# Fifteen normalising products moved from VectorE to GpSimd in a planned attention kernel, with scores two groups ahead and a new order

## The chip, the cores and the metric

The kernel runs on one core of one Trainium2 chip. The metric is the device time of one execution in microseconds. The kernel before took 671.77 us, the median of three runs (670.23, 671.77 and 672.2).

## The reference

Two independent blocks with 2048 positions, a model width of 512 and 32 heads of width 16. Their results stand side by side in the output.

```python
# A: one K and one V for all 32 heads
q = (x @ wq) as [head, position, 16];  k = x @ wk;  v = x @ wv
p = softmax(q k^T / 4)                 # 32 heads x 2048 x 2048
a = (p v) @ wo
# B: linear attention with learned features
q, k, v = x @ wqkv, by head
phi(y) = concat(softmax(y w_phi), softmax(-y w_phi))
kv = sum_s phi(k)^T v;  z = sum_s phi(k)
b = ((phi(q) kv) / (phi(q) z + 1e-6)) @ wo
out = concat(a, b)
```

## The kernel before, in words

**Block A, the large part.** The work is cut into 32 pieces `sc` (a query block of 512, a pair of heads in four row groups, the even or odd head of each pair) by 16 key blocks `kap` of 128. For each of these 512 combinations there are four score tiles `g` of 128x512, so 2048 tiles in all. TensorE makes a score tile with one matmul of 32 rows (`score`, line 1757). From there a tile goes one of two ways:

- *The ScalarE way.* Tiles are taken in groups of two, in two neighbouring PSUM banks (`next_qk`, `qk`). One activation over 128x1024 takes the exponential into the ring `PT` (`expo`, line 1824). Four such tiles are then multiplied with V by four matmuls that run side by side in four column tiles (`pv`, line 1867).
- *The VectorE way.* VectorE turns one tile at a time into 16-bit integers whose bits, read as f16, approximate the exponential (`bits`, line 1938). Four tiles make a "quad", a plane of the buffer `Z`, which has 14 planes. The approximation sums four shifted copies. GpSimd makes the second plane from the first with one 64-bit integer addition (line 1982) and the third and fourth from the first two with another one (line 2000). If GpSimd is late by the planner's reckoning (`LATE`), or near the end (`ALONE`), VectorE makes some of the planes itself (line 1985, jobs named `dS`). Each of the four planes needs four matmuls (`d_pv`, line 2036), so a quad costs TensorE 16 matmuls with V where a ScalarE quartet costs 4.

All products with V of one `sc` accumulate in PSUM bank 5, with the sum of the weights in extra columns. When an `sc` is complete, VectorE copies it out (`finish_sc`, line 1529 as "accS"), takes the reciprocal of the sums (`finish_sc2`, line 2069), the reciprocals go by DMA through DRAM into the spread-out tile `denS`, and a product normalises two `sc` at once into `On` (`finish_sc3`, line 2096; for the last even one line 2094). There are 15 such products at line 2096, one per odd `sc` below 30: 128x512 f32 times 128x512 f32 into bf16. They are jobs named `on`. The output projection, and the copying out of a piece three later, wait for them.

**Block B** is interleaved with it: projections, exponentials on ScalarE (lines 2275 and 2354), row sums and products on VectorE, and once in the middle `b_kvfin` (lines 2331 to 2346), which closes the accumulated `kv` and `z`: two products into `KVn` (line 2338) and four small ones into `KX` (line 2346).

**The order of the work.** Nothing is scheduled on the chip. At build time the class `_Fast` simulates the engines with a duration for every job (0.60 us for a VectorE tile, 0.4267 us per tile and 0.05 us for a ScalarE group, 1.135 and 2.03 us for the GpSimd additions, `ODUR` for a normalising product), picks at each step the job that can start first, and writes out one fixed instruction order for each engine. Each engine then works through its list in order and waits on semaphores. Ties and near ties are broken by priorities plus a pseudo-random amount that depends on a seed; there is one seed for each 14 us of planned time (`SEEDS`). How many tiles go to VectorE is not fixed anywhere: a VectorE score (`dq`) is issued when the rules allow it (`dq_ok`, `can_open`, `riders`). Some of these rules:

- `LOOK`: a score group `i` for ScalarE may be issued when `i <= nex + LOOK`, where `nex` is the number of exponentials issued.
- `HOLD`: a VectorE score that would not share its time on TensorE with another score is put behind other ready TensorE work unless VectorE will have been idle for `-HOLD` us at its start.
- `LAST`: in the last piece a new quad is only opened while at least this many key blocks are left.

**Locks.** An instruction added with `lock=True` on VectorE is remembered (`last_lock`), and the next locked instruction on GpSimd waits for it. GpSimd's additions are locked, as are VectorE's normalising products, its `dS` planes, the products in `b_ew`, `b_qw` and `b_kvfin`. The planner also keeps jobs in `PAIR` and GpSimd's jobs off each other in time (`paired`, `port`).

Of the kernel before, what the change touches and what calls it, by code (L numbers as in the profile page):

```python
# [1175 lines left out]
class _Fast:  # L1176
# [697 lines left out]
    def dve_quad(self):  # L1874

        for sc in (self.asc, self.asc + 1):
            if sc < 32 and ("qa", sc // 2) in self.issued and 16 - self.at[sc] - self.dt[sc] >= (self.LAST if sc == 31 else self.AHEAD) and all(("KR", sc % 2, k) in self.issued for k in range(4)):
                return sc
# [73 lines left out]
    def block(self, quad):  # L1952
# [3 lines left out]
        late = max(0.0, self.te["pool"] - self.te["dve"]) + self.pbusy + self.PDUR + self.PPAIR  # L1956
        mode = sum(late > x for x in self.LATE)
        if self.asc >= 31 and 16 - self.at[31] - self.dt[31] <= self.ALONE:
# [372 lines left out]
    def b_kvfin(self):  # L2331


        kvS, KVn, mask = self.kvS, self.KVn, self.mask
        mk = ["mask0"] + [("mask", j) for j in range(8)]
        for a in range(2):
            o = KVn.rearrange("p g (j a e) -> p a g j e", a=2, j=4)[:, a]
            self.add("dve", (lambda a, o: (lambda v: v.tensor_tensor(out=o, in0=kvS[:, :, a, 0:16].unsqueeze(2).to_broadcast([128, 8, 4, 16]),  # L2338
                                                                     in1=mask[:, a, :].unsqueeze(1).unsqueeze(3).to_broadcast([128, 8, 4, 16]), op=ALU.mult)))(a, o),
                     reads=["kvS"] + mk, writes=[("KV", a)], lock=True)  # L2340
        z = kvS[:, :, :, 16:17]
        self.add("dve", lambda v: v.tensor_scalar(out=z, in0=z, scalar1=5e-7, scalar2=None, op0=ALU.add), reads=["kvS"], writes=["kvS"])
        for sg in range(2):
            for a in range(2):
                o, i = self.kx(1 + sg, a), z[:, 4 * sg:4 * sg + 4, a, :].to_broadcast([128, 4, 4])
                self.add("dve", (lambda o, i, a: (lambda v: v.tensor_tensor(out=o, in0=i, in1=mask[:, a, :].unsqueeze(1).to_broadcast([128, 4, 4]), op=ALU.mult)))(o, i, a),
                         reads=["kvS", "KX0"] + mk, writes=[("Zc", 2 * sg + a)], lock=True)

    def b_pq(self, m, G, dc):
        return self.Wq[:, dc, G * 128:G * 128 + 128], self.BxT[:, dc, m * 512:(m + 1) * 512], [("BxT", m), ("Wq", dc)]  # L2350
# [71 lines left out]
    def b_s8c(self, st):  # L2422
# [15 lines left out]
    ACTIVE = 4.5  # L2438
    FORCE = 3.45
    SEG = 14.0  # L2440
    SEEDS = (0, 0, 123515, 372835, 67414, 19330, 290997, 497586, 506994, 1038613, 983868, 663097, 811365, 174557, 947041, 618921,
             796598, 856510, 445263, 482332, 137281, 222396, 619280, 216959, 825991, 456468, 828108, 116528, 672282, 460342, 1003417, 806511,
             80739, 543698, 705153, 314868, 260223, 835086, 464019, 411522, 111904, 658750, 941122, 672462, 101118, 679772, 19846)
    PVN = 2
    AENG, ADUR, SENG, SDUR, ONP, ODUR = 'dve', 0.6, 'dve', 1.13, 0, 0.62
    LATE = (14.0, 24.0)
    OPEN, SPARE = 2, 4
    RESV, URGE, URG2, ORD = None, 1.0, 0.8, 0.08
    PLAST, PDPV, PDQ, PPV, SAME = 0.6, 2.0, 0.4, 1.5, 0.1
# [4 lines left out]
    AMP = (0.6, 1.0, 1.4)  # L2454
    PDUR, PPAIR = 1.135, 2.03
    GS, FREE0 = (2, 2), (0, 1, 2, 3, 4, 6, 7)
    LOOK, DLA, TOL, LAG = 1, 0.3, 0.3, 0.44
    PQE, PQR, EASE = 2.2, 1.1, 0.45
    LONE, HOLD, HOLDW = 1.2, -0.4, 0.2
    PAIR = ("dS", "on", "ew")  # L2460
    LAST = 6
    ALONE = 4
    SPREAD = 5.5
    COMPANY = 4.5
# [93 lines left out]
    def seed(self, t):  # L2558

        i = int(t / self.SEG)  # L2560
        return self.SEEDS[i] if i < len(self.SEEDS) else 0

# [164 lines left out]
```

## Time and profile before

| | before |
|---|---|
| median of 3 runs | 671.77 us |
| profiled execution, its own time | 670.24 us |
| its span, first to last instruction | 668.5 us |
| granted TensorE clock | 0.999 |
| score tiles on ScalarE / on VectorE | 1340 / 708 |
| quads on VectorE | 177 |

In the rows of the profile, "x" is the number of instructions, then follow the busy time of the group in us and the mean duration of one instruction in ns, then the idle time of the engine just before them and what ended it. Consecutive instructions of one engine overlap a little, so that the busy time of a group can be less than count times mean. PE is TensorE (PEld its weight loads), DVE VectorE, ACT ScalarE, POOL GpSimd. PE's durations contain the latency of a pipelined matmul.

### The profile page before, as it was taken

What the parts mean: (1) busy time and instruction counts of PE and PEld (TensorE: products, weight loads), DVE (VectorE), ACT (ScalarE), POOL (GpSimd) and SP (SyncE); (2) the same over time, 40 slices, a digit from 0 to 9 for tenths busy, and PEclk for the clock granted to TensorE, in tenths of its full rate; (3) what the DMA queues carried; (4) which work ended last, traced back from release to release, by engine and by line L of the source; (5) the groups of instructions that cost most, each with busy time, mean ns of one, the idle gap of its engine ahead of it and who ended that gap; (6) DMA issues with size and microseconds to landing.
All of it is one profiled execution on the core that took longest, in us unless ns stands there. A gap on an engine that the chain in (4) does not pass through costs nothing.

```text
span 668.5 us, 20877 instructions
## 1 busy us (share of the span) xinstructions
PE 650.2 (97%) x9026; PEld 202.9 (30%) x9026; DVE 621.6 (93%) x1048; ACT 652.1 (98%) x742; POOL 531.4 (79%) x413
## 2 busy tenths in 40 slices
PE   8999999999999999999999999999999999999997
PEld 3332233233332233223322323233233223222232
DVE  5999999999999999999999899999978999999985
ACT  6999999999999999999999999999999999999995
POOL 5788899986778876987688898887865778878982
PEclk9999999999999999999999999999999999999999
DMA  9931000000000100000112000130210220010101
GB/s 193 158 98 26 3 11 18 3 26 4 11 19 10 50 3 12 19 3 26 31 22 57 26 26 12 29 90 15 72 51 26 73 58 26 11 49 11 26 2 37
DMA packets 45552, 24.12 MB, mean 36 GB/s; under 512 B 35404, under 2 KB 41548, under 8 KB 45452
## 3 DMA queue, kind: packets, MB, share of 16 engines
q1 hardware_dynamic: 43724, 22.43, 14.1%
q8 instruction: 71, 1.16, 0.7%
q10 hardware_dynamic: 1728, 0.30, 0.2%
q14 instruction: 29, 0.24, 0.1%
HBM read 10.27 MB, written 4.96 MB: 23 GB/s over the span
## 4 chain that ended last, share of the span: by engine, by line
ACT 82%; PE 14%; DVE 2%; DMA 1%; POOL 0%; issue 0%
ACT f_PT L1824 78%; PE f_ps L1757 4%; PE f_ps L2036 4%; PE f_ps L1354 3%; ACT f_ET L2354 2%; PE f_ps L1867 2%; ACT f_Ek L2275 2%; DVE f_Z L1938 1%; DMA f_AxT<-in_A_x_dram 1%; PE f_ps L2123 0%; POOL f_Z L2000 0%; PE f_ps L1523 0%; DVE f_KR L1709 0%; PE f_ps L1692 0%; DVE f_KVn L2338 0%
## 5 line engine op out<-in xcount | busy, mean ns | idle before, releaser
L1824 ACT ACTIVATE f_PT<-f_ps 128x1024 bf16<-128x1024 f32 x670 | 622.8, 1137 | 3.3 <-PE f_ps L1757 1.7
L1938 DVE TENSOR_SCALAR f_Z<-f_ps 128x512 int16<-128x512 f32 x708 | 444.8, 682 | 18.9 <-PE f_ps L1757 16.1
L2000 POOL INT64_ADD f_Z<-f_Z x175 | 331.0, 1892 | 34.3 <-DVE f_On L2096 5.6
L1757 PE MATMUL f_ps<-f_QA,f_KR 32*128 32x512 bf16 x2048 | 272.5, 385 | 8.4 <-ACT f_PT L1824 5.4
L1982 POOL INT64_ADD f_Z<-f_Z x175 | 181.6, 1038 | 77.8 <-DVE f_Z L1938 47.0
L2036 PE MATMUL f_ps<-f_Z,f_VK 128*32 128x512 f16 x2832 | 229.3, 384 | 2.3 <-POOL f_Z L1982 1.4
L1757 PEld LDWEIGHTS f_ps<-f_QA,f_KR 32*128 32x128 bf16 x2048 | 74.2, 91 | 253.8 <-ACT f_PT L1824 218.5
L1867 PE MATMUL f_ps<-f_PT,f_VA 128*32 128x512 bf16 x1340 | 116.3, 385 | 0.1
L2036 PEld LDWEIGHTS f_ps<-f_Z,f_VK 128*32 128x32 bf16 x2832 | 57.2, 95 | 83.7 <-issue 56.3
L1867 PEld LDWEIGHTS f_ps<-f_PT,f_VA 128*32 128x32 bf16 x1340 | 27.5, 94 | 47.8 <-issue 42.4
L2281 DVE TENSOR_REDUCE f_ssum<-f_Ek 128x64 f32<-128x1024 bf16 x16 | 19.3, 1206 | 2.2 <-ACT f_Ek L2275 2.2
L1529 DVE COPY f_accS<-f_ps 128x512 f32<-128x512 f32 x31 | 21.1, 681 | 0.1
L2298 DVE TENSOR_TENSOR f_vS<-f_ps,f_rs 128x1024 bf16<-128x1024 f32 x16 | 19.4, 1215 | 0.5 <-PE f_ps L1354 0.5
L2354 ACT ACTIVATE f_ET<-f_ps 128x512 bf16<-128x512 f32 x32 | 19.2, 739 | 0.0
L1354 PE MATMUL f_ps<-f_Wk,f_BxT 128*32 128x512 bf16 x256 | 19.0, 383 | 0.0
L1354 PE MATMUL f_ps<-f_BxT,f_Wq 128*32 128x512 bf16 x256 | 18.5, 382 | 0.2 <-ACT f_ET L2354 0.2
L1354 PE MATMUL f_ps<-f_Bwo,f_ET 128*32 128x512 bf16 x256 | 18.6, 382 | 0.0
L1354 PE MATMUL f_ps<-f_Bwv,f_BxT 128*32 128x512 bf16 x256 | 18.5, 382 | 0.0
L2275 ACT ACTIVATE f_Ek<-f_ps 128x512 bf16<-128x512 f32 x32 | 18.3, 675 | 0.0
L1354 PE MATMUL f_ps<-f_AxT,f_wq 128*32 128x512 bf16 x240 | 17.5, 382 | 0.2 <-DVE f_Z L1938 0.2
L1523 PE MATMUL f_ps<-f_ones,f_zero 128*32 128x512 bf16 (+8 forms) x98 | 13.4, 371 | 1.3 <-POOL f_zero L1549 1.3
L1354 PE MATMUL f_ps<-f_wo,f_On 128*32 128x512 bf16 x192 | 14.3, 383 | 0.0
(106 smaller groups left out, 277.9 us busy)
## 6 DMA issues: line engine op xcount, KB each, us to landing
f_denS<-f_dd SPq DMA_DIRECT2D x15, 256.0 KB
out_dram<-f_outB SPq DMA_DIRECT2D x17, 128.0 KB, 2.6
f_Wk<-f_wd SPq DMA_DIRECT2D x4, 512.0 KB
f_Ek<-f_wd SPq DMA_DIRECT2D x4, 512.0 KB
f_accS<-f_accS SPq DMA_DIRECT2D x60, 32.0 KB
out_dram<-f_outA SPq DMA_DIRECT2D x14, 128.0 KB, 1.9
f_Bwv<-in_B_wqkv_dram SPq DMA_DIRECT2D x1, 512.0 KB
f_Bwo<-in_B_wo_dram SPq DMA_DIRECT2D x1, 512.0 KB
```

The costliest lines, as they stand in the source:

```text
L1354: mm = pe.matmul(ps[32 * j:32 * j + 32, bank, :], lhsT=l[:, 32 * j:32 * j + 32], rhs=r, start=(c == 0), stop=(c == N - 1), tile_position=( ...
L1529: self.add("dve", lambda v: v.tensor_copy(out=out, in_=in_), reads=reads, writes=writes)
L1757: return pe.matmul(self.ps[:, bank, :], lhsT=self.KR[32 * g:32 * g + 32, sc % 2, kap * 128:(kap + 1) * 128], rhs=self.QA[32 * g:32 * g + 3 ...
L1824: self.add("act", lambda a: a.activation(out=PT[:, sl[0]:sl[0] + size, :], in_=ps[:, bs[0]:bs[0] + size, :], func=ACT.Exp), reads=[("PS", ...
L1867: mm = pe.matmul(ps[32 * g:32 * g + 32, bank, :], lhsT=w, rhs=PT[:, slots[g], :], start=start, stop=stop, tile_position=(0, 32 * g))
L1938: self.add("dve", lambda v: v.tensor_scalar(out=self.Z[:, z, h, :], in0=ps[:, bank, :], scalar1=self.Z1, scalar2=self.Z0, op0=ALU.mult, op ...
L1982: self.add("pool", lambda g: g.int64_add(out=w(o), in0=w(i), in1=256 * t * 0x0001000100010001), reads=keys(z), writes=keys(p), lock=True)
L2000: self.add("pool", lambda g: g.int64_add(out=v(*o), in0=v(*sorted((z, y))), in1=512 * 0x0001000100010001), reads=keys(z) + keys(y), writes ...
L2036: mm = pe.matmul(ps[32 * g:32 * g + 32, bank, :], lhsT=w, rhs=Z[:, sl[g], :], start=start, stop=stop, tile_position=(0, 32 * g))
L2275: self.add("act", (lambda a, sg: (lambda e: e.activation(out=Ek[:, r, a].rearrange("p h f -> p (h f)"), in_=ps[:, bank, :], func=ACT.Exp, ...
L2298: self.add("dve", lambda v: v.tensor_tensor(out=vS[:, :, :, 0:16], in0=v3, in1=rs.unsqueeze(3).to_broadcast([128, 2, 32, 16]), op=ALU.mult ...
L2354: self.add("act", lambda e: e.activation(out=self.ET[:, sl, :], in_=self.ps[:, bank, :], func=ACT.Exp, scale=sg), reads=[("PS", bank)], wr ...
```

## The change

The normalising products with `sc < 30` are added to GpSimd's list in place of VectorE's (`ONP` from 0 to 30), with 1.27 us planned for one instead of 0.62. The six products of `b_kvfin` are no longer locked. Score groups may stand two ahead (`LOOK`), the thresholds `LATE`, `HOLD` and `LAST` are moved, and the seeds are new ones from the third segment on, so that the fixed order of the engines' instructions is another one.

```diff
# b_kvfin
-                     reads=["kvS"] + mk, writes=[("KV", a)], lock=True)
+                     reads=["kvS"] + mk, writes=[("KV", a)])
...
-                         reads=["kvS", "KX0"] + mk, writes=[("Zc", 2 * sg + a)], lock=True)
+                         reads=["kvS", "KX0"] + mk, writes=[("Zc", 2 * sg + a)])
# constants
-    SEEDS = (0, 0, 123515, 372835, 67414, 19330, 290997, 497586, 506994, 1038613, 983868, 663097, 811365, 174557, 947041, 618921,
...
+    SEEDS = (0, 0, 167143, 130480, 298315, 266520, 1016351, 757449, 657965, 146296, 518941, 206005, 348923, 764209, 586831, 950700,
...
-    AENG, ADUR, SENG, SDUR, ONP, ODUR = 'dve', 0.6, 'dve', 1.13, 0, 0.62
-    LATE = (14.0, 24.0)
+    AENG, ADUR, SENG, SDUR, ONP, ODUR = 'dve', 0.6, 'dve', 1.13, 30, 1.27
+    LATE = (16.0, 30.0)
...
-    LOOK, DLA, TOL, LAG = 1, 0.3, 0.3, 0.44
+    LOOK, DLA, TOL, LAG = 2, 0.3, 0.3, 0.44
...
-    LONE, HOLD, HOLDW = 1.2, -0.4, 0.2
+    LONE, HOLD, HOLDW = 1.2, -0.7, 0.2
...
-    LAST = 6
+    LAST = 8
```

The lines that read `ONP` are unchanged:

```python
self.add("pool" if sc < self.ONP else "dve", lambda v: v.tensor_tensor(out=o, in0=acc, in1=R, op=ALU.mult), reads=reads, writes=[("On", sl)], lock=True)
```

More of the change, by code (lines that the diff above doesn't have):

```diff
@@ L2440 @@
     SEG = 14.0
-    SEEDS = (0, 0, 123515, 372835, 67414, 19330, 290997, 497586, 506994, 1038613, 983868, 663097, 811365, 174557, 947041, 618921,
-             796598, 856510, 445263, 482332, 137281, 222396, 619280, 216959, 825991, 456468, 828108, 116528, 672282, 460342, 1003417, 806511,
-             80739, 543698, 705153, 314868, 260223, 835086, 464019, 411522, 111904, 658750, 941122, 672462, 101118, 679772, 19846)
+    SEEDS = (0, 0, 167143, 130480, 298315, 266520, 1016351, 757449, 657965, 146296, 518941, 206005, 348923, 764209, 586831, 950700,
+             639825, 267858, 893993, 668738, 464524, 750513, 225125, 193461, 0, 648673, 371881, 500552, 497624, 251567, 487201, 114980,
+             171633, 94996, 831771, 817116, 897134, 587649, 526128, 870704, 1011496, 896371, 868450, 261383, 0, 529598, 955066)
     PVN = 2
-    AENG, ADUR, SENG, SDUR, ONP, ODUR = 'dve', 0.6, 'dve', 1.13, 0, 0.62
-    LATE = (14.0, 24.0)
+    AENG, ADUR, SENG, SDUR, ONP, ODUR = 'dve', 0.6, 'dve', 1.13, 30, 1.27
+    LATE = (16.0, 30.0)
     OPEN, SPARE = 2, 4
```

## The prediction

> **What bounds the kernel now.** I read the page first: the busy shares, the chain that ended last, the costliest groups.
>
> ```profile
> span 668.5 us, 20877 instructions
> PE 650.2 (97%) x9026; PEld 202.9 (30%) x9026; DVE 621.6 (93%) x1048; ACT 652.1 (98%) x742; POOL 531.4 (79%) x413
> ACT 82%; PE 14%; DVE 2%; DMA 1%; POOL 0%; issue 0%
> L1824 ACT ACTIVATE f_PT<-f_ps 128x1024 bf16<-128x1024 f32 x670 | 622.8, 1137 | 3.3 <-PE f_ps L1757 1.7
> L1938 DVE TENSOR_SCALAR f_Z<-f_ps 128x512 int16<-128x512 f32 x708 | 444.8, 682 | 18.9 <-PE f_ps L1757 16.1
> L2000 POOL INT64_ADD f_Z<-f_Z x175 | 331.0, 1892 | 34.3 <-DVE f_On L2096 5.6
> L1982 POOL INT64_ADD f_Z<-f_Z x175 | 181.6, 1038 | 77.8 <-DVE f_Z L1938 47.0
> ```
>
> ScalarE carries the chain (82%) and stands only 3.3 us before its 670 score exponentials. Busy time of TensorE is no measure of its load, since the latency of pipelined matmuls is in it. Next the stretches, and the start and end of ScalarE's row in the timeline:
>
> ```profile
> core 0: us, PE busy (x) PEld busy (x) DVE busy (x) ACT busy (x) POOL busy (x), PEclk, DMA share, GB/s
> 40.00:240.00 200.00, 197.70 (x2906) 61.35 (x2898) 195.72 (x318) 199.92 (x230) 169.10 (x124) 1.00 0.06 15
> 240.00:440.00 200.00, 195.81 (x2792) 60.88 (x2792) 189.68 (x315) 197.88 (x229) 163.44 (x115) 1.00 0.10 26
> 440.00:540.00 100.00, 98.56 (x1406) 31.33 (x1396) 90.31 (x146) 99.99 (x117) 71.17 (x48) 1.00 0.20 53
> 540.00:640.00 100.00, 97.94 (x1217) 28.50 (x1219) 95.60 (x165) 99.62 (x110) 86.16 (x60) 1.00 0.08 24
> ```
>
> ```profile
> 8.36 3.91 ACT L1824 ACTIVATE f_PT<-f_ps 128x1024 bf16<-128x1024 f32 x4 [0.65 <-PE f_ps L1757]
> ```
>
> ```profile
> 649.00 9.50 ACT L1824 ACTIVATE f_PT<-f_ps 128x1024 bf16<-128x1024 f32 x10
> ```
>
> ```profile
> 562.96 72.63 ACT f_PT L1824 x79
> ```
>
> From 40 to 640 us ScalarE is busy for 597.4 of 600 us. The run is therefore a start of 8.36 us before the first score exponential, a solid block to 649.00 + 9.50 = 658.5, and a tail of 10.0 us. Only fewer exponentials shorten the block; the chain's stretch of 79 gives 72.63 / 79 = 0.92 us for each. VectorE is the engine that can take them over: it is full from 40 to 240 us (195.72 of 200), and has 2 to 10% left later. One quad more on VectorE is four score tiles, or two exponentials: **1.84 us less on ScalarE**. That is the exchange rate of this forecast.
>
> **The change, part by part.**
>
> *The products leave VectorE.*
>
> ```profile
> L2096 DVE TENSOR_TENSOR f_On<-f_accS,f_denS 128x512 bf16<-128x512 f32 x15 | 14.3, 954 | 0.0
> ```
>
> ```profile
> L2096 DVE TENSOR_TENSOR f_On<-f_accS,f_denS x15: 679/686/1957, 71.5 to 645.3; 128x512 bf16<-128x512 f32 x15
> ```
>
> VectorE is rid of 14.3 us. At the median of 686 ns the fifteen would be 10.3 us; the other 4.0 us belong to a few that took up to 1957 ns. [...]
>
> What the freed time buys: a VectorE tile costs 444.8 / 708 = 0.628 us, a quad 2.51. A quad also shortens the run by 1.84 us, and with it VectorE's own room by 93% of that, 1.71 us. So 14.3 us buy 14.3 / (2.51 + 1.71) = 3.4 quads, or 6.2 us; 10.3 us buy 2.4 quads, or 4.5 us. The order, however, is laid out with the planner's figures, 0.62 us for a product and 0.60 for a tile: 9.3 / (2.40 + 1.71) = 2.3. I take **two quads, 3.7 us**.
>
> *The products arrive on GpSimd.* The trace shows no two-operand product there. The nearest rows:
>
> ```profile
> L1585 POOL COPY f_wk_rep<-f_wk_raw 128x512 bf16<-128x512 bf16 x1 | 0.6, 609 | 1.6 <-DMA f_wk_raw<-in_A_wk_dram 1.6
> ```
>
> A copy of 512 elements takes 0.61 us; an addition over 512 words of 64 bits, which reads the same 4 KB of each partition as two f32 operands, 1.04; one over twice as much 1.89. I take 1.2, nearest to the 1.04 with a second stream to fetch, and keep 0.61 to 1.89. [...]
>
> ```profile
> POOL f_Z L2000 <- DVE f_On L2096: 5.6, 8, 0.8
> POOL f_Z L1982 <- DVE f_On L2096: 1.7, 2, 1.0
> POOL f_Z L1982 <- DVE f_KX L2346: 2.0, 1, 2.0
> POOL f_Z L1982 <- DVE f_Z L1938: 47.0, 50, 6.9
> ```
>
> GpSimd gets 15 x 1.2 = 18 us (9 to 28) and loses the locked waits on the product, 5.6 + 1.7 = 7.3 us, so some 11 us in all. Two quads bring 2 x (1.04 + 1.89) = 5.9 us. It would then be busy for 531.4 + 18 + 5.9 = 555 of about 665 us, 84%. Its slack covers that: of its idle time 47.0 us alone are spent waiting for VectorE's tiles. If the cover were gone, the following would stand behind a product: the next additions in GpSimd's list, the products with V that need their planes in TensorE's list, and behind these the scores for ScalarE. TensorE waits little for additions so far:
>
> ```profile
> PEld f_ps L2036 <- POOL f_Z L1982: 5.1, 15, 1.7
> PEld f_ps L2036 <- POOL f_Z L2000: 4.1, 15, 0.5
> ```
>
> Without any cover it would be the whole 18 us. I put the term at nothing, since the planner places a product at 1.27 us, above the price I take, and since one score group in hand covers 0.92 us.
>
> *TensorE for two more quads.*
>
> ```profile
> 299.66 1.04 PE L2036 MATMUL f_ps<-f_Z,f_VK 128*32 128x512 f16 x16
> 301.82 0.39 PE L2036 MATMUL f_ps<-f_Z,f_VK 128*32 128x512 f16 x4
> ```
>
> Four matmuls side by side follow each other at (1.04 - 0.39) / 3 = 0.22 us. A quad needs four such groups where ScalarE's quartet needs one, so 0.65 us more; two quads 1.3 us on an engine that also loses 3.7 us of span. That is 5 us, 0.7%. The order finds it from the looser `LOOK`, or it doesn't; this is the first rival.
>
> *Score groups two ahead.* The exponentials' idle time is 3.3 us in all, so this can give ScalarE no more than that. On the other side, three groups hold six of the seven banks that are free for anything but the sums. What that costs VectorE is bounded by the waits for scores it has now, 16.1 us; I take nothing for it, and leave it to the last rival.
>
> *The end.* `LAST` at 8 can leave one quad less to VectorE, 1.84 us lost. In return the end can close sooner:
>
> ```profile
> 657.15 1.89 POOL L2000 INT64_ADD f_Z<-f_Z  x1 [2.45 <-DVE f_Z L1985]
> 658.95 0.39 PE L1867 MATMUL f_ps<-f_PT,f_VA 128*32 128x512 bf16 x4
> 660.03 0.60 PE L2036 MATMUL f_ps<-f_Z,f_VK 128*32 128x512 f16 x8
> ```
>
> The last planes come from GpSimd at 659.04 and are used up at 660.63, while ScalarE's last tiles are through at 659.34: up to 1.3 us to gain. Between -1.3 and +1.8 I take nothing.
>
> *The unmarked closing.* One wait of 2.0 us on GpSimd goes. Now its addition and a product into `KVn` may collide, and VectorE may lose what it lost at line 2096, 1957 - 686 = 1.27 us, at each of two products. Once in 668 us and off ScalarE's path: nothing, at worst 2.5 us of VectorE, which is 0.6 quads or 1.1 us.
>
> `LATE` concerns planes that VectorE makes because GpSimd is late:
>
> ```profile
> L1985 DVE TENSOR_SCALAR f_Z<-f_Z x6: 679/684/1787, 649.7 to 656.4; 128x2048 int16<-128x2048 int16 x6
> ```
>
> There are six, all after 649 us, so the thresholds hardly ruled before: nothing.
>
> **The sum.** The profiled execution took 670.24 us, 1.74 more than its span. Two quads less for ScalarE: 670.24 - 3.7 = 666.5. The median of the runs lies 1.53 us above the profiled one, so for it **671.77 - 3.7 = 668.1 us**.
>
> **The rivals.**
>
> *Nothing is converted.* The products alone, by stretch:
>
> ```profile
> 40.00:240.00 200.00, 2.97 (x4) 1.00 0.06 15
> ```
>
> VectorE is relieved, but what kept quads from it after 240 us was not its own time: it had 10.3 us free from 240 to 440 and 9.7 from 440 to 540, while TensorE was as good as full. Four products fall before 240 us. Then only the 40 to 240 stretch converts, under 4 x 0.74 = 3.0 us, or 0.7 quads. The seeds may change which stalls the plan has, but ScalarE has none to give on the chip. Time: 671.77 within 1.3, so 670.5 to 673. [...]
>
> *All of it is converted.* 14.3 us for 3.4 quads, and the 1.3 us of the end: 671.77 - 7.5 = 664.3. For it speaks that the planner was wrong by 15 x (0.954 - 0.62) = 5 us on these products and is no longer; against it, that it does not know so when it lays out the order.
>
> *Slower: `HOLD` eats the gain.*
>
> ```profile
> DVE f_Z L1938 <- PE f_ps L1757: 16.1, 45, 1.6
> ```
>
> VectorE waits 45 times for a score, 0.36 us on average, which is about the 0.4 us that `HOLD` asks it to stand before a lone score. With 0.7 each wait can grow by 0.3 us: 45 x 0.3 = 13.5 us, more than the planned 9.3 that are freed. The balance of -4.2 us is one quad less (4.2 / 4.11), `LAST` takes another, and ScalarE gets four exponentials more: 671.77 + 3.7 = 675.5. It decides once these waits exceed 16.1 + 9.3 = 25.4 us. Against it: `HOLD` only reorders scores behind other ready work, and the third group gives lone scores more company to ride with.
>
> **How the numbers follow.** About 0.3%, 2.0 us, is what a measurement of this kernel can tell from no change. I give the two quads 0.47, everything converted 0.11, nothing converted 0.24, slower by `HOLD` 0.18. The forecast's own spread, a quad either way, is 666.2 to 670.0, all but its last 0.2 us beyond the bound. Faster is thus 0.58, same 0.24, slower 0.18. The range runs from 664.0, which takes in the full conversion, to 674.0, which takes in the nothing case and one quad lost; beyond lie the larger losses and a still better order.
>
> **What would show it.** In the changed profile line 1938 should have about 716 instructions in place of 708, line 1824 about 666, and line 2096 fifteen on POOL at about 1.2 us, with VectorE's busy time near 621.6 - 14.3 + 8 x 0.628 = 612 and GpSimd's near 555. ScalarE's idle time before its exponentials should stay under 5 us; if instead it grows, the products stand in front of planes (line 2036 waiting for POOL far above 9.2 us) or the banks are short. A count of 708 or less at line 1938 makes the forecast wrong at its conversion; waits of line 1938 for scores over 25 us name `HOLD`. With the counts as forecast and the time not lower, the tail or the start has grown, and the exchange rate was no rate of the whole run.

## The result and the profile after

The changed kernel takes 872.54 us, the median of six runs (869.21 to 880.52), beside 671.52 for the kernel before on the same chips: 1.300 times as long, 95% interval 1.297 to 1.303. The forecast of 668.1 was wrong in sign and by 204 us. The profiled execution took 869.21 us.

The page of the changed kernel, busy shares, chain and costliest groups:

```profile
span 867.5 us, 20854 instructions
PE 693.0 (80%) x8976; PEld 202.9 (23%) x8976; DVE 614.7 (71%) x1037; ACT 657.7 (76%) x740; POOL 553.7 (64%) x430
PE 27%; ACT 26%; issue 20%; POOL 15%; DVE 11%; DMA 1%; POOLq 0%
L1824 ACT ACTIVATE f_PT<-f_ps 128x1024 bf16<-128x1024 f32 x668 | 627.8, 1103 | 185.7 <-PE f_ps L1757 185.0
L1938 DVE TENSOR_SCALAR f_Z<-f_ps 128x512 int16<-128x512 f32 x712 | 448.8, 683 | 205.0 <-PE f_ps L1757 191.5
L2000 POOL INT64_ADD f_Z<-f_Z x176 | 333.1, 1893 | 63.7 <-issue 28.8
L2036 PE MATMUL f_ps<-f_Z,f_VK 128*32 128x512 f16 x2848 | 250.7, 410 | 149.3 <-POOL f_Z L1982 113.5
L1982 POOL INT64_ADD f_Z<-f_Z x176 | 182.9, 1039 | 111.4 <-issue 58.5
L2096 POOL TENSOR_TENSOR f_On<-f_accS,f_denS 128x512 bf16<-128x512 f32 x15 | 18.8, 1255 | 105.3 <-issue 98.5
```

The engines' work is near what was forecast: VectorE and GpSimd are busy for 615 and 554 us (612 and 555 forecast), and ScalarE for 658, where it was 652 before. The span is longer because ScalarE stands for 185.7 us before its score exponentials, where it stood for 3.3. It waits for scores; TensorE, which makes them, stands for 149.3 us before its products with V (line 2036), most of it for GpSimd's planes. And the three groups of GpSimd show a sort of idle time that they did not have before: "issue", time in which the engine waits for nothing that the profile shows. It is 98.5 us before the products, and 58.5 + 28.8 us before the additions that follow them. GpSimd's row in the timeline shows it at the first product:

```profile
68.24 1.89 POOL L2000 INT64_ADD f_Z<-f_Z  x1
76.82 1.26 POOL L2096 TENSOR_TENSOR f_On<-f_accS,f_denS 128x512 bf16<-128x512 f32 x1 [6.69 <-issue]
83.86 1.03 POOL L1982 INT64_ADD f_Z<-f_Z  x1 [5.78 <-issue]
```

From 70.13 to 83.86 us GpSimd does one product of 1.26 us. The lists of lines 2096, 1982 and 2000 (duration minimum/median/maximum in ns, then the first and last start in us) name what stands in front of the gaps:

```profile
L2096 POOLq MODIFY_POOL_CONFIG  x30: 10/11/11, 70.1 to 824.2; - x30
L2096 POOL TENSOR_TENSOR f_On<-f_accS,f_denS x15: 1252/1253/1270, 76.8 to 831.4; 128x512 bf16<-128x512 f32 x15
```

```profile
L1982 POOLq MODIFY_POOL_CONFIG  x22: 1/1/11, 21.4 to 832.9; - x22
```

```profile
L2000 POOLq MODIFY_POOL_CONFIG  x10: 1/1/1, 188.0 to 791.5; - x10
```

Those are 62 instructions on GpSimd's queue, two for each of 31 changes: one at the start, and fifteen to a product and fifteen back to the additions. Nobody wrote them into the kernel. The trace of the kernel before had them too, once, ahead of its first addition:

```profile
L1982 POOLq MODIFY_POOL_CONFIG  x2: 11/11/11, 21.3 to 21.4; - x2
```

The first change of the run, behind the copies at its start, stops nothing. The addition after it begins 0.20 us after the last copy, in the kernel before as in the changed one:

```profile
21.58 1.04 POOL L1982 INT64_ADD f_Z<-f_Z  x1 [0.20 <-DVE f_Z L1938]
```

So the instructions mark a change, and what a change costs has to be read at the gap behind them. Why the first one is free is not shown.

The moment of the first product on the other engines (the timeline of the changed kernel):

```profile
77.35 0.40 PE L2036 MATMUL f_ps<-f_Z,f_VK 128*32 128x512 f16 x4
84.94 0.62 PE L2036 MATMUL f_ps<-f_Z,f_VK 128*32 128x512 f16 x4 [7.19 <-POOL f_Z L1982]
86.14 1.02 ACT L1824 ACTIVATE f_PT<-f_ps 128x1024 bf16<-128x1024 f32 x1 [7.48 <-PE f_ps L1757]
86.17 0.69 DVE L1938 TENSOR_SCALAR f_Z<-f_ps 128x512 int16<-128x512 f32 x1 [7.28 <-PE f_ps L1757]
```

TensorE comes to a product with V whose plane isn't there and stands for 7.19 us; the scores of both other engines are behind it in its list. The stretches of this place have a second loss, in the column PEclk:

```profile
core 0: us, PE busy (x) PEld busy (x) DVE busy (x) ACT busy (x) POOL busy (x), PEclk, DMA share, GB/s
78.10:86.10 8.00, 1.16 (x11) 0.29 (x11) 0.79 (x2) 0.56 (x1) 2.07 (x2) 0.66 0.00 0
86.10:90.00 3.90, 1.72 (x43) 0.53 (x43) 0.69 (x1) 1.02 (x1) 3.57 (x3) 0.50 0.00 0
90.00:95.00 5.00, 5.00 (x45) 0.86 (x42) 3.46 (x7) 3.39 (x4) 4.48 (x4) 0.56 0.03 5
95.00:100.00 5.00, 5.00 (x68) 1.38 (x64) 4.69 (x8) 5.00 (x6) 4.56 (x4) 1.00 0.00 0
```

After the stop TensorE has half its clock until about 95 us. Over the whole run the granted clock is 0.879, before it was 0.999.

### The profile page after: what moved, and what is told of

It reads as the page before. It is cut to its first block, busy times and chain, and to the rows that moved or that the text cites. A ratio compares the mean times of both kernels' runs of the same rounds, so it can differ in the third digit from the quotient of the medians.

```text
span 867.5 us, 20854 instructions
## 1 busy us (share of the span) xinstructions
PE 693.0 (80%) x8976; PEld 202.9 (23%) x8976; DVE 614.7 (71%) x1037; ACT 657.7 (76%) x740; POOL 553.7 (64%) x430
## 4 chain that ended last, share of the span: by engine, by line
PE 27%; ACT 26%; issue 20%; POOL 15%; DVE 11%; DMA 1%; POOLq 0%
ACT f_PT L1824 24%; PE f_ps L1757 9%; PE f_ps L2036 8%; POOL f_Z L2000 8%; DVE f_Z L1938 6%; PE f_ps L1354 5%; POOL f_Z L1982 5%; PE f_ps L1867 3%; POOL f_On L2096 2%; ACT f_Ek L2275 1%; ACT f_ET L2354 1%; DVE f_vS L2298 1%; DVE f_ssum L2281 1%; DMA f_AxT<-in_A_x_dram 1%; DVE f_accS L1529 1%
## 5 line engine op out<-in xcount | busy, mean ns | idle before, releaser
L1824 ACT ACTIVATE f_PT<-f_ps 128x1024 bf16<-128x1024 f32 x668 | 627.8, 1103 | 185.7 <-PE f_ps L1757 185.0
L2000 POOL INT64_ADD f_Z<-f_Z x176 | 333.1, 1893 | 63.7 <-issue 28.8
L2036 PE MATMUL f_ps<-f_Z,f_VK 128*32 128x512 f16 x2848 | 250.7, 410 | 149.3 <-POOL f_Z L1982 113.5
L1757 PE MATMUL f_ps<-f_QA,f_KR 32*128 32x512 bf16 x2048 | 282.3, 404 | 5.7 <-ACT f_PT L1824 3.5
L1982 POOL INT64_ADD f_Z<-f_Z x176 | 182.9, 1039 | 111.4 <-issue 58.5
L1867 PE MATMUL f_ps<-f_PT,f_VA 128*32 128x512 bf16 x1336 | 120.4, 404 | 0.1
L2096 POOL TENSOR_TENSOR f_On<-f_accS,f_denS 128x512 bf16<-128x512 f32 x15 | 18.8, 1255 | 105.3 <-issue 98.5
L1354 PE MATMUL f_ps<-f_BxT,f_Wq 128*32 128x512 bf16 x256 | 20.7, 420 | 0.1
L1354 PE MATMUL f_ps<-f_Bwo,f_ET 128*32 128x512 bf16 x256 | 20.8, 408 | 0.0
L1529 DVE CAST f_outA<-f_ps 128x512 bf16<-128x512 f32 x14 | 9.5, 681 | 13.3 <-PE f_ps L1354 13.3
```

Of the source, the lines that this page charges most:

```text
L1354: mm = pe.matmul(ps[32 * j:32 * j + 32, bank, :], lhsT=l[:, 32 * j:32 * j + 32], rhs=r, start=(c == 0), stop=(c == N - 1), tile_position=( ...
L1529: self.add("dve", lambda v: v.tensor_copy(out=out, in_=in_), reads=reads, writes=writes)
L1757: return pe.matmul(self.ps[:, bank, :], lhsT=self.KR[32 * g:32 * g + 32, sc % 2, kap * 128:(kap + 1) * 128], rhs=self.QA[32 * g:32 * g + 3 ...
L1824: self.add("act", lambda a: a.activation(out=PT[:, sl[0]:sl[0] + size, :], in_=ps[:, bs[0]:bs[0] + size, :], func=ACT.Exp), reads=[("PS", ...
L1867: mm = pe.matmul(ps[32 * g:32 * g + 32, bank, :], lhsT=w, rhs=PT[:, slots[g], :], start=start, stop=stop, tile_position=(0, 32 * g))
L1982: self.add("pool", lambda g: g.int64_add(out=w(o), in0=w(i), in1=256 * t * 0x0001000100010001), reads=keys(z), writes=keys(p), lock=True)
```

## The experiments

Three theories. **Theory A**: every alternation between the 64-bit addition and the f32 product stops GpSimd for 6 to 7 us (5.7 to 7.6 in the trace of the changed kernel), whatever the size of the instruction. The expectations call this an exchange of code; that is the author's assumption, no run shows what happens in the stop. **Theory B**: the place of the products in GpSimd's list, with what they wait for, makes the planes late. **Theory C**: the new order (two groups ahead, longer hold) lets TensorE starve and its clock drop.

**e1: the order untouched, copies in place of the products.** The normalisation of these fifteen is left out.

```diff
-        self.add("pool" if sc < self.ONP else "dve", lambda v: v.tensor_tensor(out=o, in0=acc, in1=R, op=ALU.mult), ...)
+        if sc < self.ONP:
+            for _ in range(2):
+                self.add("pool", lambda v: v.tensor_copy(out=o, in_=acc), reads=reads, writes=[("On", sl)], lock=True)
+            return
...
```

> The changed kernel, its order and waits untouched, but each of the fifteen products on GpSimd is replaced by two copies of 128x512 f32 to bf16 (the multiplication by the reciprocal sums is left out there). Two copies should hold GpSimd about as long as one product, 1.2 to 1.4 us. Theory A (GpSimd has to exchange its code between the product and the 64-bit addition, 5.8 to 7.0 us each way): copies need no exchange, so the time falls from 872.5 to 666 to 670. Theory B (the place of the products in GpSimd's list, with their waits for the reciprocals, makes the planes late): the time stays at 840 to 875. Theory C (the new order itself lets TensorE's clock drop): stays above 850.

Measured: 671.28 us, ratio to before 0.9997 (0.9986 to 1.0008). GpSimd's rows:

```profile
L2000 POOL INT64_ADD f_Z<-f_Z x176 | 333.2, 1893 | 30.8 <-DVE f_ET L2409 7.5
L1982 POOL INT64_ADD f_Z<-f_Z x176 | 182.6, 1038 | 54.2 <-DVE f_Z L1938 28.4
L2098 POOL CAST f_On<-f_accS 128x512 bf16<-128x512 f32 x30 | 18.4, 612 | 3.3 <-POOL f_Z L2000 1.9
```

Thirty copies hold GpSimd for 18.4 us, as long as the fifteen products did (18.8), in the same places, behind the same waits. The "issue" time is gone and with it 201.3 us, and the trace has two MODIFY_POOL_CONFIG in place of 62. Theories B and C fall. It is 1 to 5 us slower than the 666 to 670 that I expected of A; e8 and e9 find why.

**e2: the order untouched, the products back on VectorE.**

```diff
-        self.add("pool" if sc < self.ONP else "dve", lambda v: v.tensor_tensor(
+        self.add("dve", lambda v: v.tensor_tensor(
```

> The changed kernel's order with only the engine of the fifteen products put back to VectorE, at the place in VectorE's list that follows from the same plan. Theory A: no exchange of code is left, 668 to 673, the products costing VectorE 10 to 14 us that the plan does not know of. Theory B: about the same, 668 to 673. Theory C (the order, with two groups ahead and the longer hold): stays above 850.

Measured: 676.54 us, ratio 1.0074 (1.0061 to 1.0087); 3.5 us above the expected range. This order was laid out without the products on VectorE: there they cost 676.54 - 671.28 = 5.3 us.

**e3: five of the fifteen on GpSimd.**

```diff
-        self.add("pool" if sc < self.ONP else "dve", lambda v: v.tensor_tensor(
+        self.add("pool" if sc < self.ONP and sc % 6 == 5 else "dve", lambda v: v.tensor_tensor(
```

> The changed kernel's order, with five of the fifteen products on GpSimd and ten put back to VectorE. Theory A: each product on GpSimd costs the run the same, 200 us / 15 = 13.3 us, so 670 + 5 x 13.3 = 737, within 10. Theory B, if lateness builds up on GpSimd from one product to the next: less than a third of the loss, under 715. Theory C: above 850.

Measured: 741.1 us. Counted from e2, which has none, that is 64.6 / 5 = 12.9 us for each; with all fifteen it is (872.54 - 676.54) / 15 = 13.1. The loss is proportional to the count, and so are the MODIFY_POOL_CONFIG: 22, two at the start and four for each product.

**e4: the kernel before, with fifteen products of one element per partition added.**

```diff
         self.add("pool" if sc < self.ONP else "dve", lambda v: v.tensor_tensor(out=o, in0=acc, in1=R, ...
+        if self.rec is None and sc < 30:
+            self.add("pool", lambda g: g.tensor_tensor(out=self.half2, in0=self.half2, in1=self.half2, op=ALU.mult), writes=["half2"])
```

> The kernel before, products on VectorE as they were, with fifteen additional products of one element per partition on GpSimd, one at each product's place, with no data from or for anything else. Theory A: the exchange does not depend on the size, so 671.5 + 15 x 12 = 850, between 820 and 870. Theory B: fifteen tiny instructions of 0.2 us cost nothing, 671 to 676. Theory C: nothing, 671 to 674.

Measured: 856.92 us, ratio 1.278 (1.275 to 1.280), or 185.7 / 15 = 12.4 us for each. Their row:

```profile
L2100 POOL TENSOR_TENSOR f_half<-f_half 128x1 f32<-128x1 f32 x15 | 2.7, 183 | 105.0 <-issue 105.0
```

Work of 2.7 us with no part in the computation, in the kernel before with its own order, makes 185.7 of the 201 us. The size of the product hardly matters: a product of 512 elements costs 12.9 to 13.1 us, one of a single element 12.4. The two are measured in different orders, so the rest of 15 us is not traced to anything.

**e5: one such product** (`sc == 13` only in the line above).

> The kernel before with a single additional one-element product on GpSimd, in the middle of the run. Theory A (two exchanges of code per product, each for itself): 671.3 + 12.4 = 683.7, the 12.4 us being a fifteenth of what the fifteen tiny products cost; between 681 and 686. Rival (a first exchange is dearer, or the cost comes only when exchanges are repeated): above 690 or below 676.

Measured: 685.7 us, ratio 1.0223 (1.0202 to 1.0243): 14.9 us for a single one. It costs no less alone than as one of fifteen.

**e7: two of them at each of the fifteen places**, one behind the other.

> As the fifteen tiny products, but two of them one behind the other at each of the fifteen places, thirty in all. Theory A (the cost is the alternation between two sorts of GpSimd code, not the product): only 15 x 0.2 to 0.4 us more than the fifteen, 858 to 865. Rival (each such product costs its own 12 us): about 1040.

Measured: 866.82 us (two runs), 9.9 us more than with one; slightly above what I expected, and far from 1040. GpSimd in the timeline, and the list of the first of the two lines:

```profile
80.07 0.18 POOL L2100 TENSOR_TENSOR f_half<-f_half 128x1 f32<-128x1 f32 x1 [7.47 <-issue]
80.33 0.19 POOL L2101 TENSOR_TENSOR f_half<-f_half 128x1 f32<-128x1 f32 x1
86.31 1.89 POOL L2002 INT64_ADD f_Z<-f_Z  x1 [5.78 <-issue]
```

```profile
L2100 POOLq MODIFY_POOL_CONFIG  x30: 9/11/13, 72.6 to 826.8; - x30
```

The second one follows after 0.08 us, and line 2101, which is its line, has no MODIFY_POOL_CONFIG. What costs is the alternation, 7.47 us there and 5.78 us back. Of the 9.9 us, the second products explain 15 x 0.27 = 4.0; the stops before the first ones are 3.7 us longer in all than in e4 (108.7 against 105.0), and the rest is open.

**e6: idle matmuls where TensorE stands**, in the changed kernel, to see what the lower clock costs.

```diff
...
+        if self.rec is None and p in self.late:    # p: written by the first addition behind a product
+            self.late = set()
+            self.fill(cols=(512,) * 32, start=start, mode="col", bank=bank)
```

> The changed kernel with the same order, plus 32 groups of four idle matmuls of 512 columns (zero weights, about 6.8 us) ahead of the first product with V that waits for an addition behind each product on GpSimd, so that TensorE is busy while it would stand. Theory A1 (the stop alone makes the loss, the lower clock after it is hidden): no gain, 872 to 885. Theory A2 (TensorE comes back at half clock after a stop and loses 3 us or more each time): 15 x 3 = 45 us less, 815 to 845.

Measured: 893.82 us, 21.3 us more than the changed kernel; neither expectation held. But the edit does not do at every place what it was meant to do. At three of the fifteen, the plane that TensorE waits for is not the marked one, so it stands all the same and runs the idle matmuls (the fill) afterwards. One of them:

```profile
199.58 1.04 PE L2044 MATMUL f_ps<-f_Z,f_VK 128*32 128x512 f16 x8 [11.23 <-POOL f_Z L1985]
201.52 8.56 PE L1524 MATMUL f_ps<-f_ones,f_zero 128*32 128x512 bf16 x128
```

The stretches from one product to the next are longer by 5.7, 7.4 and 7.7 us at these three places, 20.8 of the 25.1 us by which the profiled span grew. At the other twelve they differ by -1.1 to +2.1 us. The first of these, in the stretches shown above for the changed kernel:

```profile
78.10:86.10 8.00, 7.24 (x131) 3.25 (x123) 0.83 (x2) 0.59 (x1) 1.90 (x3) 1.00 0.01 2
86.10:90.00 3.90, 1.07 (x43) 0.49 (x40) 0.69 (x1) 1.02 (x1) 3.57 (x4) 0.81 0.00 0
90.00:95.00 5.00, 5.00 (x41) 0.84 (x37) 3.01 (x6) 3.07 (x3) 4.48 (x4) 0.50 0.03 5
```

The clock was 1.00 while the fill ran. But a second wait for GpSimd follows, for a cast of the linear part; the changed kernel has it too, of 2.18 us:

```profile
89.33 0.42 PE L2326 MATMUL f_ps<-f_vS,f_Ek 128*32 128x34 bf16 x32 [2.83 <-POOL f_vS L2314]
```

From 90 to 95 us the clock was 0.50 all the same. At two places the fill outlasted the stop, and TensorE went on behind it without standing. The nine microseconds behind the stop at one of them, in the changed kernel and then in e6:

```profile
470.85:479.85 9.00, 8.95 (x102) 2.62 (x102) 3.86 (x7) 5.12 (x5) 6.90 (x5) 0.50 0.08 21
492.70:501.70 9.00, 9.00 (x164) 3.24 (x160) 6.46 (x12) 8.20 (x9) 6.19 (x6) 1.00 0.22 61
```

Here the clock stays at 1.00 and ScalarE does 3.1 us more work (8.20 against 5.12 us). But TensorE goes on 3.0 us after the first addition behind the product has ended (at 489.69 us), where the changed kernel goes on at once, and the stretch to the next product lasts as long as without the fill (52.39 against 52.57 us). So e6 does not separate the two. The pages allow an estimate. For e1, the same order without the alternation, the page has:

```profile
PE 650.3 (97%) x8976; PEld 201.3 (30%) x8976; DVE 612.6 (92%) x1037; ACT 651.0 (97%) x740; POOL 553.0 (83%) x445
```

With the same 8976 matmuls, TensorE in the changed kernel is busy for 693.0 - 650.3 = 42.7 us longer, and the other 155.5 us of the difference between the spans (867.5 and 669.3) it stands. By this, about 10.4 of the 13 us for each product are the stop and 2.8 slower matmuls. That a full clock would save these 2.8 us **is not shown**.

**e8: only the closing unmarked**, in the kernel before; the order of every engine is the same.

```diff
-                     reads=["kvS"] + mk, writes=[("KV", a)], lock=True)
+                     reads=["kvS"] + mk, writes=[("KV", a)])
...
-                         reads=["kvS", "KX0"] + mk, writes=[("Zc", 2 * sg + a)], lock=True)
+                         reads=["kvS", "KX0"] + mk, writes=[("Zc", 2 * sg + a)])
```

> The kernel before, same order, with only the six products of the closing no longer locked. Theory: a GpSimd addition and one product into KVn collide, the product takes up to 2.5 us in place of 0.69, GpSimd's wait of 2.0 us goes; ScalarE does not see it, the time is the same within 0.2%, 670 to 673. Rival (the unmarked collisions cost several microseconds): above 674.

Measured: 673.02 us, ratio 1.0037 (1.0025 to 1.0050): 2.2 us, between the two expectations. Here is the place, first in the kernel before:

```profile
309.39 1.29 DVE L2338 TENSOR_TENSOR f_KVn<-f_kvS,f_mask 128x512 bf16<-128x512 f32 x2
310.71 0.18 DVE L2342 TENSOR_SCALAR f_kvS<-f_kvS 128x16 f32<-128x16 f32 x1
310.93 0.44 DVE L2346 TENSOR_TENSOR f_KX<-f_kvS,f_mask 128x16 bf16<-128x16 f32 x4
313.32 4.86 ACT L1824 ACTIVATE f_PT<-f_ps 128x1024 bf16<-128x1024 f32 x5 [1.00 <-PE f_ps L1757]
```

and in e8:

```profile
309.87 1.53 DVE L2338 TENSOR_TENSOR f_KVn<-f_kvS,f_mask 128x512 bf16<-128x512 f32 x1
310.94 2.20 POOL L2000 INT64_ADD f_Z<-f_Z  x1
311.43 1.75 DVE L2342 TENSOR_SCALAR f_kvS<-f_kvS 128x16 f32<-128x16 f32 x1
313.21 0.43 DVE L2346 TENSOR_TENSOR f_KX<-f_kvS,f_mask 128x16 bf16<-128x16 f32 x4
314.30 0.41 PE L2365 MATMUL f_ps<-f_ET,f_KX 128*32 128x128 bf16 x16 [2.04 <-DVE f_Z L1938]
315.19 1.02 ACT L1824 ACTIVATE f_PT<-f_ps 128x1024 bf16<-128x1024 f32 x1 [2.08 <-PE f_ps L1757]
```

The tiny line 2342 takes 1.75 us beside an addition, where it took 0.18. `KX` is ready at 313.64 in place of 311.37, and the conversions behind it on VectorE (line 1938) are as late. TensorE stands 2.04 us at the matmul that reads `KX`; the profile names the first of these conversions as what released it. ScalarE misses a score for 2.08 us and in the next two steps for 0.49 and 0.50 us, 3.07 us in all where it stood for 1.00 before: that is nearly all of the 2.2 us.

**e9: e1 with the closing locked again.**

> As the kernel with two copies in place of each product (same order; the multiplication by the reciprocal sums is left out there), with the six products of the closing locked again. Theory: unmarking the closing cost 2.2 us in the kernel before and costs the same here, so 671.3 - 2.2 = 669.1, between 668 and 670; the order without the exchange of code is then faster than before by 0.3%. Rival (the marking only shifts where GpSimd waits, in this order it hits nothing): 671 to 672.

Measured: 669.05 us, ratio 0.9961 (0.9947 to 0.9975). So unmarking costs the new order 671.28 - 669.05 = 2.2 us as well. ScalarE's score exponentials, and its wait in the tail:

```profile
L1824 ACT ACTIVATE f_PT<-f_ps 128x1024 bf16<-128x1024 f32 x668 | 622.1, 1123 | 1.4 <-PE f_ps L1757 0.8
ACT f_ET L2140 <- DVE f_ET L2138: 4.3, 1, 4.3
```

The first and the last of the exponentials:

```profile
8.64 1.94 ACT L1824 ACTIVATE f_PT<-f_ps 128x1024 bf16<-128x1024 f32 x2 [0.65 <-PE f_ps L1757]
```

```profile
649.73 5.67 ACT L1824 ACTIVATE f_PT<-f_ps 128x1024 bf16<-128x1024 f32 x6
```

The block now lasts from 8.64 to 655.40, or 646.8 us, 3.4 less than before (650.1). But the tail from 655.40 to the end of the span at 667.4 takes 12.0 us in place of 10.0, since the closing of the last piece comes later behind the last exponential (4.3 us of waiting before line 2140, before 2.7).

**e10: e2 with the closing locked again.**

> The changed kernel's order with the fifteen products back on VectorE and the six products of the closing locked again, which leaves of the change only the new order, two groups ahead among it. Theory: 676.5 - 2.2 = 674.3, between 673 and 675.5, still slower than before since the order was laid out without the products on VectorE. Rival (marking changes nothing here): 676 to 677.

Measured: 672.9 us, ratio 1.0027 (1.0017 to 1.0036), 3.6 us less than e2, somewhat better than expected, and 3.9 us more than e9. No kernel with all of the products beats the kernel before.

**The account**, by medians, beginning with the kernel before at 671.2: the new order, with the products' time on GpSimd but without alternation, -2.1 (e9); unmarking the closing, +2.2 (e1); the alternation with the products, +201.3 (the changed kernel).

## Why the prediction was wrong, point by point

*The step that failed* is the term for the products' arrival on GpSimd, which was put at nothing: "I put the term at nothing, since the planner places a product at 1.27 us, above the price I take, and since one score group in hand covers 0.92 us." The price of the product was right: 1.2 forecast, 1.255 measured, within 0.61 to 1.89; and GpSimd is busy for 553.7 us where 555 were forecast. But the sum counted the instruction alone. The change from the addition to the product and back, 6.5 to 7.6 us and 5.7 to 6.0 in the changed kernel, isn't in any duration. It made the term 201.3 us. Even the bound for the case without cover, "the whole 18 us", was low by a factor of eleven. e1, e3, e4 and e7 show it: no loss without the alternation, loss in proportion to its number, and hardly any dependence on the size. The path was named rightly, additions, then products with V, then scores, and so was its sign, "line 2036 waiting for POOL far above 9.2 us"; what was missing is the time that stands on it.

There was a hint, but no price with it. The list of line 1982 in the trace of before has two MODIFY_POOL_CONFIG ahead of the first addition, and the addition begins 0.20 us after the last copy: nothing in that trace says that such a change can cost more, or that a product and an addition make one. The price came only with the product on GpSimd: 5.7 to 7.6 us each way in the changed kernel, 14.9 us for a single product of one element per partition in e5.

*The rivals.* None of them is the cause. For the slower one, `HOLD`: in e1, the same order without the alternation, VectorE waits 22.9 us for scores, more than the 16.1 before, but under the 25.4 at which that rival was to decide.

*The exchange rate and the conversion.* ScalarE was the bound, and in e9 its block shortens by 3.4 us, near the 3.7 of the forecast, but not by two quads: there is one (712 tiles at line 1938, 668 exponentials at line 1824; forecast 716 and 666), worth 1.84 us, and the exponentials' idle time fell from 3.3 to 1.4 us, a gain that I had bounded at 3.3 and put at nothing. That the two add up to the forecast's 3.7 is luck.

*The end* was put at nothing between -1.3 and +1.8; e9's tail is 2.0 us longer, just outside.

*The unmarked closing* was put at nothing, at worst 1.1 us, because it lies "off ScalarE's path". It costs 2.2. That VectorE can lose 1.27 us or more beside an addition was right (line 2342 lost 1.57); the error was the path: TensorE's list has a matmul there that waits for VectorE, and scores stand behind it. The wait of 2.0 us that the lock put on GpSimd was the cheaper place for it.

*VectorE's relief* was right in size. It is busy for 614.7 us, with 612 forecast; the forecast had two quads in it, and with one it would be 609.8. In e9 it is 610.6, so nearly all of the 14.3 us are gone. That the excess over the median, 4.0 us, would go with the products has a ground in the trace of before: the seven stretched ones, of 0.93 to 1.96 us, each begin while a GpSimd addition is running, the longest of them here:

```profile
312.60 1.90 POOL L2000 INT64_ADD f_Z<-f_Z  x1
313.08 1.96 DVE L2096 TENSOR_TENSOR f_On<-f_accS,f_denS 128x512 bf16<-128x512 f32 x1
```

The rival that nothing is converted was given a time of 670.5 to 673. The measured time is far from it, for a reason that this rival doesn't contain. Without the alternation and with the lock, the new order with copies in the products' place is 0.4% faster than the kernel before (e9) and 0.6% faster than with the products on VectorE (e10), so there the work was better off on GpSimd.

## What to carry to other kernels

Before moving an instruction to GpSimd, look not only at its duration there but at what runs before and after it on that engine: an alternation between the 64-bit additions and a product cost 12 to 15 us a time here, whether the instruction was worth 1.26 us or 0.18. MODIFY_POOL_CONFIG on the queue and, behind it, idle time put down to "issue" are its marks. A pair without such a gap, as at the start of the trace of before, is no cost yet. A single instruction of the new sort, as in e5, shows the price before fifteen are moved. An operation that takes a lock off is priced by who waits for its engine in another engine's in-order list, not by whether its own engine is the bound.

## What the runs showed of the hardware

The thirty copies of e1 (CAST in its rows) alternate with the 64-bit additions on GpSimd without a stop: 3.3 us of idle time before all thirty, none of it "issue". F32 products do not: 98.5 us of "issue" before the fifteen of the changed kernel. The stop there is somewhat longer towards the product (6.5 to 7.6 us) than back to the addition (5.7 to 6.0 us). Two products in a row share one stop, the second follows after 0.08 us (e7). At the change at the start of the run, from copies to the addition, the gap was 0.20 us. After TensorE had stood for 7.19 us its granted clock was 0.50 to 0.56 for the next 9 us; a wait of 2.83 us after a fill at 1.00 was followed by 0.50 from 90 to 95 us, and from 492.70 to 501.70 us, where the fill left no wait, the clock stayed at 1.00 (e6). A VectorE instruction of 16 elements per partition took 1.75 us in place of 0.18 while a GpSimd addition ran beside it, and the addition 2.20 in place of 1.89 (e8).
